# Attention plus gated expert on one Trainium2 core: expert matmuls in 128x32 column strips behind value passes, four products in one PSUM bank

## The chip, the cores and the metric

The kernel runs on one core of one Trainium2 chip, in one launch. The metric is the device time of one execution in microseconds (us); it is given as the median of several runs. The profile is that of one execution.

## The reference

Inputs are `q`, `k` and `v` of shape (8 batches, 12 heads, 448 tokens, 64) and two weights, `w_in` (768 x 2048) and `w_out` (2048 x 768), all in float32.

```
scores = q k^T / 8          per batch and head, 448 x 448
attn   = softmax(scores)
x      = attn v             heads side by side: 3584 tokens x 768
h      = x w_in             3584 x 2048
g      = h * sigmoid(h)
out    = g w_out            3584 x 768, float32
```

## The kernel before

All matmuls are in float16, with float32 sums in PSUM. The kernel is one long list of instructions whose order is made at build time: a planner (`Order`, with `Op`s that carry an estimated duration, dependences and a bias) plays the five engines forward and writes down what each does next. Rings (`Ring`) stand for buffers: an operation may start when a ring has a free entry. Each engine then works through its own list strictly in order, and waits on semaphores where data or a buffer is not ready. TensorE (PE) chooses between three kinds of work: score passes (`run_qk`), value passes (`run_av`) and a list `moe` of expert matmuls, of which any ready one among the first 24 may go.

Three shapes of matmul use the 128x128 array differently.

- **Scores** (`scores`, `scores_rest`, L336): contraction over 32 rows, so four heads run side by side in row tiles (32 x 128). A score pass has 8 matmuls of 448 columns (two rounds of four). ScalarE (ACT) takes the exponential of the scores (`expo`, L373).
- **Value passes** (`attend`, `attend_sums`, L399 and L415): output over 32 columns of the array, so four heads run side by side in column tiles (128 x 32). From the second batch on, units (a batch and a group of four heads) go in pairs. Part 0 sums the exponentials; parts 1 and 2 give the even and the odd half of the head dimension. A pair has three chunks of keys of its own for each unit, and one chunk in which the lower 64 rows belong to one unit and the upper 64 to the other ("the rest", 64 x 32 tiles). In each of parts 1 and 2 the own chunks come first and the shared chunk last: six rounds of four matmuls and one round of eight.
- **Expert matmuls** use the whole array: `ffn1` (L496, `h = x w_in`, six matmuls of 448 columns for each of 16 slices `f` of the 2048), `plain` (L718, the first four output tiles), `product` (L704) and `pair_product` (L632).

The second expert matmul is done for two tiles of 128 tokens at a time (a "quad", `queue_quad`) by Strassen's scheme: seven products of half size instead of eight. The inputs of the products are sums of quarters of `g` (`combine_g`, L694, on VectorE, DVE) and of `w_out` (`combine_w`, L533). Each product is eight matmuls of 384 columns. Products 3 and 5, 4 and 2, and 1 and 7 share a PSUM bank (the later one adds on top), product 6 has its own. `take_3`, `take_5` and `take_2` are copies on ACT (L770, L776, L780); `take_4`, `take_1`, `less_12`, `less_21`, `take_6` and `take_7` are additions on DVE (L766). Finished tiles lie in `ost` buffers (four) and are stored by SyncE's queue, in part by ACT's towards the end.

The first expert matmul of the last two batches is done by a seven-product scheme too (`queue_pair`, `pair_product`): for each of eight `f`, products 1, 6, 7, 5, 2, 3, 4 of three matmuls each. Its inputs are sums of `x` (`combine_x`, `sx`, L590) and of `w_in` (`combine_w_in`, `tw`, L608), its results are added on DVE (`pair_add`, L663), copied on ACT (`pair_copy`, L657) and gated on ACT (`silu`, L670). The buffer of `sx` 3 is the one that held `V` of the last batch. The normalised `x` of a value pass is written by DVE (`norm`, L482).

What a batch needs before its `ffn1` or its pair stage may run is the `norm` of its last value pass. Up to there the planner fills PE with products of older quads.

Of the kernel before, what the change touches and what calls it, by code (L numbers as in the profile page):

```python
# [165 lines left out]
def kernel(  # L166
# [36 lines left out]
    SHY = 0.5  # L203
    FAR = (NT * B // 4 - 3, NT * B // 4 - 1)
# [4 lines left out]
    NSG, NTMP, NOST = 3, 3, 4  # L209
# [213 lines left out]
    def attend(ns, part):  # L423
        made = []
        lone = len(ns) == 1
        if part == 0 and not lone:
            attend_sums(ns)
            return
        for n in ns:
            a = ps.tile([128, 512], FP32, name=f"a_{n}_{part}", tag="m", bufs=4)  # L430
            made.append(a)
            acc[(n, part)] = a
            for c in range(NCH if lone else NCH - 1):
                for h in range(HG):
                    attend_mm(
                        a, n, part, c, h, 0, rows_of(n, c), E[(n, c // per_burst(n))],
                        c == 0, lone and c == NCH - 1,
                    )
        if not lone:
            for h in range(HG):  # L440
                for i, n in enumerate(ns):
                    attend_mm(
                        made[i], n, part, 3, h, 64 * i, 64 * (i + 1), E[(ns[0], 3)],
                        False, True,
                    )

# [43 lines left out]

    h_t, th_t, o_t = {}, {}, {}

    def ffn1(b, f, t0, t1):
        h = ps.tile([128, 512], FP32, name=f"h_{b}_{f}_{t0}", tag="m", bufs=4)
        for cc in range(NDC):
            nc.tensor.matmul(  # L496
                out=h[:, 0 : t1 - t0],
                lhsT=w_in_t[:, cc, 128 * f : 128 * (f + 1)],
                rhs=x3(b, cc)[:, cc % 3, t0:t1],
                start=(cc == 0),  # L500
                stop=(cc == NDC - 1),
            )
        h_t[(b, f, t0)] = h
# [13 lines left out]
    W_ = {m: const.tile([128, HF, OH], FP16, name=f"D{m}") for m in (1, 4, 6)}  # L517
# [5 lines left out]
    W_[3], W_[7], W_[5], W_[2] = B_[0, 1], B_[1, 0], B_[1, 1], B_[0, 0]  # L523

    def combine_w(m, f0, f1):
        i0, i1, op = {
            1: ((0, 0), (1, 1), ALU.add),
            4: ((1, 0), (0, 0), ALU.subtract),
            6: ((0, 0), (0, 1), ALU.add),
            3: ((0, 1), (1, 1), ALU.subtract),  # L530
            7: ((1, 0), (1, 1), ALU.add),
        }[m]
        nc.vector.tensor_tensor(  # L533
            out=W_[m][:, f0:f1], in0=B_[i0][:, f0:f1], in1=B_[i1][:, f0:f1], op=op
# [76 lines left out]
    PBANK = {1: "A", 2: "A", 6: "B", 5: "C", 3: "C", 7: "D", 4: "D"}  # L611

    def pair_product(f, m):
        if m in (1, 5):
            pp_t[(f, PBANK[m])] = ps.tile(
                [128, 512], FP32, name=f"f_{f}_{m}", tag="m", bufs=4
            )[:, 0:S]
        elif m == 6:
            two = ps.tile([128, 2, 512], FP32, name=f"f_{f}_{m}", tag="s", bufs=2)
            pp_t[(f, "B")], pp_t[(f, "D")] = two[:, 0, 0:S], two[:, 1, 0:S]  # L620
# [10 lines left out]
        for c in range(3):  # L631
# [4 lines left out]
                start=(c == 0 and m in (1, 6, 5, 7)),  # L636
# [4 lines left out]
    def pair_tmp(f, name):  # L641
# [4 lines left out]
            "v": ("T", NT_, [128, HG, S], FP16),  # L646
# [4 lines left out]
        elif len(shape) == 3:  # L651
            t = t.rearrange("p h s -> p (h s)")
# [6 lines left out]
    def pair_add(f, to, x, y):  # L659
        x = pp_t[(f, x)] if x in "BCD" else pf_t[(f, x)]  # L660
        y = pf_t[(f, y)]
        out = pf_t[(f, to)] if (f, to) in pf_t else pair_tmp(f, to)
        nc.vector.tensor_tensor(out=out, in0=x, in1=y, op=ALU.add)  # L663
# [13 lines left out]
    S_t, tmp_t, ost_t, pr_t = {}, {}, {}, {}  # L677

    def combine_g(qd, m, f0, f1):
        a, b = 2 * qd, 2 * qd + 1  # L680
        x, y, op = {
            5: (rows(a, 0), rows(a, 1), ALU.add),
            2: (rows(b, 0), rows(b, 1), ALU.add),
            1: (rows(a, 0), rows(b, 1), ALU.add),
            6: (rows(b, 0), rows(a, 0), ALU.subtract),
            7: (rows(a, 1), rows(b, 1), ALU.subtract),
        }[m]
        if m > 5:
            dst = x
        else:  # L690
            if (qd, m) not in S_t:
                S_t[(qd, m)] = sb.tile([128, HF, 128], FP16, name=f"S_{qd}_{m}", tag="S", bufs=NSG)
            dst = S_t[(qd, m)]
        nc.vector.tensor_tensor(out=dst[:, f0:f1], in0=x[:, f0:f1], in1=y[:, f0:f1], op=op)  # L694

    BANK = {3: 3, 5: 3, 4: 4, 2: 4, 1: 1, 7: 1, 6: 6}

    def product(qd, m):
        w = {3: rows(2 * qd, 0), 4: rows(2 * qd + 1, 1), 6: rows(2 * qd + 1, 0), 7: rows(2 * qd, 1)}
# [3 lines left out]
        for f in range(HF):  # L703
            nc.tensor.matmul(  # L704
                out=pr_t[(qd, BANK[m])][:, 0:OH],
                lhsT=w[:, f, :],
                rhs=W_[m][:, f, :],
                start=(f == 0 and BANK[m] == m),
                stop=(f == HF - 1),
                skip_group_check=True,  # L710
            )


    def plain(t, j, f0, f1):
        if f0 == 0:
            pr_t[("o", t, j)] = ps.tile([128, 512], FP32, name=f"o_{t}_{j}", tag="m", bufs=4)
        for f in range(f0, f1):
            nc.tensor.matmul(  # L718
                out=pr_t[("o", t, j)][:, 0:OH],
                lhsT=rows(t, f // HF)[:, f % HF, :],  # L720
                rhs=B_[f // HF, j][:, f % HF, :],
                start=(f == 0),
                stop=(f == NFF - 1),
                skip_group_check=True,
# [8 lines left out]

    def tmp(qd, name):
        tmp_t[(qd, name)] = sb.tile([128, OH], FP32, name=f"{name}_{qd}", tag="tmp", bufs=NTMP)
        return tmp_t[(qd, name)]
# [28 lines left out]
    def add(out, a, b, op=ALU.add):  # L765
        nc.vector.tensor_tensor(out=out, in0=a, in1=b, op=op)  # L766


    def take_3(qd):
        nc.scalar.copy(out=tmp(qd, "s"), in_=bank(qd, 3))  # L770

    def take_4(qd):
        add(tmp_t[(qd, "s")], bank(qd, 4), tmp_t[(qd, "s")])

    def take_5(qd):
        nc.scalar.copy(out=ost(qd, 0, 1), in_=bank(qd, 3))  # L776
        store(qd, 0, 1)

    def take_2(qd):
        nc.scalar.copy(out=ost(qd, 1, 0), in_=bank(qd, 4))  # L780
        store(qd, 1, 0)

    def take_1(qd):
        add(tmp(qd, "m"), bank(qd, 1), tmp_t[(qd, "s")])

    def less_12(qd):
        add(tmp_t[(qd, "s")], tmp_t[(qd, "s")], ost_t[(qd, 0, 1)], ALU.subtract)

    def less_21(qd):
        add(tmp_t[(qd, "m")], tmp_t[(qd, "m")], ost_t[(qd, 1, 0)], ALU.subtract)  # L790

    def take_6(qd):
        add(ost(qd, 1, 1), bank(qd, 6), tmp_t[(qd, "m")])
        store(qd, 1, 1)

    def take_7(qd):
        add(ost(qd, 0, 0), bank(qd, 1), tmp_t[(qd, "s")])
        store(qd, 0, 0)
# [113 lines left out]
    sg_ring, tmp_ring, ost_ring = Ring(NSG), Ring(NTMP), Ring(NOST)  # L912
    far_ring = Ring(NX3)
    STORE = 3.0
    pr_op, sg_op, w_op, plain_op = {}, {}, {2: [], 5: []}, {}
    inv_op, norm_op = [], []
    quads = []

    def queue_ffn1(b, g0, g1):
        t0, t1 = 32 * g0, 32 * g1  # L920
        for f in range(NFF) if b == 0 else [x for f in range(HF) for x in (f, f + HF)]:

            def run(f=f):
                op = Op("PE", NDC * mm(t1 - t0), lambda: ffn1(b, f, t0, t1), tail=PE_OUT)
# [4 lines left out]
                od.on_pe(op, "full")  # L929
# [14 lines left out]
            def deps(f=f):  # L944
# [3 lines left out]
                for qd in range(NT * B // 4) if u else ():  # L948
                    if any(t // NT == u - 1 and (r or t % NT < 4) for t in (2 * qd, 2 * qd + 1)):
# [3 lines left out]
                            else [pr_op.get((qd, m)) for m in (3, 4, 6, 7)]  # L953
# [56 lines left out]
    def queue_pair_f(f, xs):  # L1010
        done, lo = {}, f // 4 * 4

        def free(r):
            made = []
            for qd in range(NT * B // 4):
                for t in (2 * qd, 2 * qd + 1):
                    if t // NT == PB // 2 - 1 and t % NT < (4, NT - 1)[r]:
                        made += [pr_op.get((qd, m)) for m in (3, 4, 6, 7)]
# [10 lines left out]
        def queue(m):  # L1029
            rings = {  # L1030
                1: ((rq_ring, 1),),
                6: ((s_ring, 1), (kt_ring, 1), (t_ring, 1)),
                5: ((rk_ring, 1),),
            }.get(m, ())
            ms = (6, 7) if m == 6 else (m,)

            def run():
                op = Op(
                    "PE",
                    3 * len(ms) * mm(S),  # L1040
                    lambda: [pair_product(f, x) for x in ms],
                    tail=PE_OUT,
                )
                if m in (1, 5):
# [7 lines left out]
                elif m == 6:  # L1052
                    read("u", "DVE", lambda: pair_add(f, "u", "B", "p"), [op, done["p"]])
                    read("v", "DVE", lambda: pair_add(f, "v", "D", "u"), [op, done["u"]])
                elif m == 5:
                    read("q", "ACT", lambda: pair_copy(f, "q", "C"), [op], None, -3)
                    read("22", "DVE", lambda: pair_add(f, "v", "q", "v"), [done["v"], done["q"]], rk_ring.give)
                    gate_of(1, 1, "v", [done["22"]], t_ring.give)
                elif m == 2:
                    gate_of(0, 0, "A", [op], m_ring.give)  # L1060
                elif m == 3:
                    read("12", "DVE", lambda: pair_add(f, "p", "C", "u"), [op, done["u"]], m_ring.give)
                    gate_of(1, 0, "p", [done["12"]], rq_ring.give)
                else:
                    read("21", "DVE", lambda: pair_add(f, "u", "D", "u"), [op, done["12"]], s_ring.give)
                    gate_of(0, 1, "u", [done["21"]], kt_ring.give)

            def deps():
                made = [xs[0, c] for c in (range(3, NDC) if m == 2 else range(3))]
                if m in (5, 6):  # L1070
                    made += [pair_x[i] for i in ((2, 3) if m == 6 else (1,))]
# [512 lines left out]
```

## Time and profile before

| | |
|---|---|
| time, median of 3 runs | 396.12 us (396.03 to 396.42) |
| span of the profiled execution, first to last instruction | 394.4 us |
| PE busy | 386.5 us (98%) |
| DVE busy | 311.3 us (79%) |
| ACT busy | 243.2 us (62%) |
| mean granted TensorE clock | 0.998 |
| bytes moved, mean | 87 GB/s |

The profiled execution is known by its span, 394.4 us; the median of the runs stands 1.7 us above it, for what lies before the first and behind the last instruction. In the timeline a row gives the start and the length of a run of equal instructions; the next row's start minus this row's start is what the run took of PE's time, since ends overlap the next start. Matmul names are output<-inputs, then the part of the array in use (128*128 whole, 32*128 row tile, 128*32 column tile), then the moving operand.

### The profile page before, as it was taken

How to read it: one execution, taken by the hardware profiler on the slowest of the kernel's cores; microseconds unless marked ns; L12 is line 12 of the kernel's file. 1: busy time of each engine (PE TensorE's matmuls, PEld its weight loads, DVE VectorE, ACT ScalarE, POOL GpSimd, SP SyncE). 2: the span in 40 equal slices, each digit the busy share in tenths (PEclk: the TensorE clock that was granted, in tenths of full speed). 3: DMA queues.
4: the chain of work that ended last, by engine and by line, in shares of the span. 5: the costliest groups of instructions: out<-in, count | busy, mean ns of one | idle time of the engine just before them, and what ended most of it. 6: DMA issues, size and time to landing. Idle time of an engine off the chain costs nothing.

```text
span 394.4 us, 9273 instructions
## 1 busy us (share of the span) xinstructions
PE 386.5 (98%) x3679; PEld 199.0 (50%) x3679; DVE 311.3 (79%) x653; ACT 243.2 (62%) x378; POOL 83.6 (21%) x153
## 2 busy tenths in 40 slices
PE   7999999999999999999999999999999999999995
PEld 6667764443444444554444444344444555556663
DVE  2466676999999697896888786988879898787863
ACT  4988885696863868626868429686593227872110
POOL 6632546315004242500051221120000000000000
PEclk9999999999999999999999999999999999999999
DMA  7999999919034863582145751531100131001334
GB/s 113 205 210 210 166 179 164 175 36 141 1 76 88 142 95 47 75 158 71 25 49 81 139 109 46 71 48 42 42 1 2 40 87 35 2 1 42 80 82 121
DMA packets 35356, 34.44 MB, mean 87 GB/s; under 512 B 11376, under 2 KB 33776, under 8 KB 35312
## 3 DMA queue, kind: packets, MB, share of 16 engines
q0 software_dynamic: 24784, 22.82, 39.2%
q1 hardware_dynamic: 9952, 10.33, 9.6%
q10 hardware_dynamic: 576, 0.69, 0.6%
q8 instruction: 29, 0.48, 0.5%
q14 instruction: 15, 0.12, 0.1%
HBM read 45.61 MB, written 11.01 MB: 144 GB/s over the span
## 4 chain that ended last, share of the span: by engine, by line
PE 94%; DMA 3%; DVE 1%; ACT 1%; POOL 0%; issue 0%; POOLq 0%
PE p L704 29%; PE h L496 29%; PE s L336 12%; PE a L399 10%; PE f L632 8%; PE o L718 3%; DMA rq<-in_q_dram 3%; PE a L415 2%; PE z L1491 1%; ACT E L373 0%; DVE S L694 0%; POOL rk L249 0%; DVE rq L323 0%; DVE rdn L466 0%; DVE ost L766 0%
## 5 line engine op out<-in xcount | busy, mean ns | idle before, releaser
L373 ACT ACTIVATE E<-s 128x896 f16<-128x896 f32 (+1 forms) x172 | 150.0, 915 | 48.6 <-PE s L336 47.5
L496 PE MATMUL h<-xT,w_in_t 128*128 128x448 f16 (+1 forms) x672 | 118.6, 327 | 0.0
L496 PEld LDWEIGHTS <-w_in_t 128*128 128x128 f16 x672 | 61.2, 98 | 54.0 <-issue 18.0
L507 ACT ACTIVATE th<-h 128x448 f16<-128x448 f32 (+1 forms) x112 | 54.3, 495 | 31.4 <-PE h L496 22.5
L543 DVE SCALAR_TENSOR_TENSOR G<-th,h 128x448 f16<-128x448 f16 (+2 forms) x112 | 55.1, 507 | 15.3 <-ACT th L507 13.3
L270 POOL DMA_DIRECT2D V<-in_v_dram x88 | 48.5, 568 | 56.5 <-PE a L399 42.7
L336 PE MATMUL s<-rq,KT 32*128 32x448 f16 (+4 forms) x768 | 50.9, 337 | 1.4 <-DVE rq L323 0.9
L704 PEld LDWEIGHTS <-G 128*128 128x128 f16 x384 | 36.5, 98 | 28.1 <-issue 4.4
L704 PEld LDWEIGHTS <-S 128*128 128x128 f16 x312 | 29.3, 98 | 23.9 <-issue 5.2
L399 PE MATMUL a<-E,V 128*32 128x448 f16 (+3 forms) x864 | 40.4, 335 | 0.0
L255 POOL DMA_DIRECT2D rq<-in_q_dram x27 | 15.1, 560 | 113.0 <-PE s L336 82.9
L704 PE MATMUL p<-D,G 128*128 128x384 f16 x208 | 37.6, 326 | 0.0
L704 PE MATMUL p<-w_out_t,S 128*128 128x384 f16 x208 | 37.2, 326 | 0.1
L482 DVE SCALAR_TENSOR_TENSOR xT<-a,rdn 128x448 f16<-128x448 f32 (+1 forms) x54 | 28.7, 565 | 7.4 <-PE a L399 6.5
L336 PEld LDWEIGHTS <-KT 32*128 32x128 f16 (+2 forms) x864 | 17.5, 98 | 29.6 <-issue 25.9
L704 PE MATMUL p<-w_out_t,G 128*128 128x384 f16 x176 | 31.9, 326 | 0.0
L399 PEld LDWEIGHTS <-V 128*32 128x32 f16 (+2 forms) x864 | 18.2, 95 | 22.4 <-issue 14.7
L384 DVE TENSOR_TENSOR T<-T,E 128x1792 f16<-128x1792 f16 x20 | 21.8, 1089 | 8.0 <-ACT E L373 7.9
L694 DVE TENSOR_TENSOR S<-G 128x512 f16<-128x512 f16 x70 | 25.3, 414 | 3.2 <-PE p L704 3.0
L384 DVE TENSOR_TENSOR T<-E,E 128x1792 f16<-128x1792 f16 x20 | 21.6, 1082 | 5.6 <-ACT E L373 5.6
L776 ACT COPY ost<-p 128x384 f32<-128x384 f32 x13 | 6.2, 480 | 27.4 <-PE p L704 22.6
L305 DVE STREAM_TRANSPOSE KT<-rk 128x256 f32<-128x256 f32 (+3 forms) x48 | 16.6, 384 | 7.0 <-DMA rk<-in_k_dram 6.2
(74 smaller groups left out, 370.2 us busy)
## 6 DMA issues: line engine op xcount, KB each, us to landing
out_dram<-ost SPq DMA_DIRECT2D x194, 48.0 KB, 1.7
rk<-in_k_dram POOLq DMA_DIRECT2D x24, 224.0 KB, 5.9
rq<-in_q_dram POOLq DMA_DIRECT2D x21, 224.0 KB, 5.2
w_in_t<-in_moe_w_in_dram POOLq DMA_DIRECT2D x6, 512.0 KB, 11.2
w_out_t<-in_moe_w_out_dram POOLq DMA_DIRECT2D x4, 768.0 KB, 13.5
V<-in_v_dram POOLq DMA_DIRECT2D x43, 64.0 KB, 3.9
V<-in_v_dram POOLq DMA_DIRECT2D x40, 48.0 KB, 4.0
out_dram<-ost SPq DMA_DIRECT2D x8, 96.0 KB, 2.2
```

What stands on the lines that cost most here:

```text
L270: nc.gpsimd.dma_start(out=VT[b][32 * x : 32 * (x + 1), hs, 0:count, :], in_=v[b, hs].rearrange("h (i g) d -> i h g d", g=TPP)[:, :, first ...
L336: nc.tensor.matmul(out=pS[p0 : p0 + 32 * (x1 - x0), h % 2, at : at + nq], lhsT=KT[(b, hg)][32 * h : 32 * (h + 1), c, x0:x1, :, e], rhs=QT[ ...
L373: nc.scalar.activation(out=E[(n, w)][0:kr, 2 * y : 2 * y + 2, 0:nk], in_=pS_t[(n, w, y)][0:kr, :, 0:nk], func=AF.Exp, scale=attn_scale,)
L384: nc.vector.tensor_tensor(out=T[n], in0=T[n] if step else E[(n, 0)], in1=E[(n, step + 1)], op=ALU.add,)
L399: nc.tensor.matmul(out=a[32 * h : 32 * (h + 1), 0:nq], lhsT=w, rhs=e[k0:k1, h, at : at + nq], start=start, stop=stop,)
L482: nc.vector.scalar_tensor_tensor(out=x3(b, cc)[:, cc % 3, 32 * g0 : 32 * g1], in0=acc[(n, part)][:, 0:nq], scalar=0.5, in1=rdn_t[n].rearra ...
L496: nc.tensor.matmul(out=h[:, 0 : t1 - t0], lhsT=w_in_t[:, cc, 128 * f : 128 * (f + 1)], rhs=x3(b, cc)[:, cc % 3, t0:t1], start=(cc == 0), s ...
L507: nc.scalar.activation(out=th, in_=h_t[(b, f, t0)][:, 0 : t1 - t0], func=AF.Tanh)
L543: nc.vector.scalar_tensor_tensor(out=dst[:, f, at + lo : at + hi], in0=th_t[(b, f, t0)][:, lo - t0 : hi - t0], scalar=1.0, in1=h_t[(b, f, ...
L632: nc.tensor.matmul(out=pp_t[(f, PBANK[m])], lhsT=w[:, c, :], rhs=a[:, c, :], start=(c == 0 and m in (1, 6, 5, 7)), stop=(c == 2), skip_gro ...
L694: nc.vector.tensor_tensor(out=dst[:, f0:f1], in0=x[:, f0:f1], in1=y[:, f0:f1], op=op)
L704: nc.tensor.matmul(out=pr_t[(qd, BANK[m])][:, 0:OH], lhsT=w[:, f, :], rhs=W_[m][:, f, :], start=(f == 0 and BANK[m] == m), stop=(f == HF - 1),
```

## The change

1. **Strips.** A new helper `times` issues an expert matmul either whole or as four matmuls of 128 x 32, one for each strip of 32 output rows. `ffn1`, `plain` and `product` are issued in strips if the last thing on PE was in column tiles (`od.mode == "cols"`) and attention work is still left.
2. **Shared keys first in part 2.** The second value pass of a pair (part 2) begins with the shared chunk; part 1 still ends with it. A value pass thus ends in 128 x 32 tiles after part 2.
3. **Another scheme for the seven products** (Winograd's form). Products 1, 6, 7 and 4 of a quad add up in one PSUM bank and are read between; 5 and 3 share a second, 2 has a third. Sums of inputs build on each other (5, then 6, then 3 and, in place, 7). Out of PSUM go four copies on ACT (`take_copy`) and three additions on DVE (`take_sum`). Three `tmp` buffers go; `ost` has seven buffers instead of four. The pair stage does the same with half of an `s` tile for products 1, 6, 7, 4: order 1, 5, 6, 2, 7, 3, 4, three copies on ACT and three additions on DVE for each `f`.
4. **A value pass gives way** to an expert matmul if a score pass is due within 0.8 us (`AWAIT`).

```diff
+    AWAIT = 0.8
-    NSG, NTMP, NOST = 3, 3, 4
+    NSG, NOST = 3, 7
...
+        if not lone and part == 2:
+            rest()
+        for i, n in enumerate(ns):
+            for c in range(NCH if lone else NCH - 1):
...
+        if not lone and part == 1:
+            rest()
...
+    def times(out, w, x, start, stop, strips):
+        cut = 32 if strips else 128
+        for i in range(0, 128, cut):
+            nc.tensor.matmul(
+                out=out[i : i + cut],
+                lhsT=w[:, i : i + cut],
+                rhs=x,
+                start=start,
+                stop=stop,
+                skip_group_check=True,
+            )
...
-            5: (rows(a, 0), rows(a, 1), ALU.add),
-            2: (rows(b, 0), rows(b, 1), ALU.add),
-            1: (rows(a, 0), rows(b, 1), ALU.add),
-            6: (rows(b, 0), rows(a, 0), ALU.subtract),
-            7: (rows(a, 1), rows(b, 1), ALU.subtract),
+            5: (rows(b, 0), rows(b, 1), ALU.add),
+            6: (S_t.get((qd, 5)), rows(a, 0), ALU.subtract),
+            7: (rows(a, 0), rows(b, 0), ALU.subtract),
+            3: (rows(a, 1), S_t.get((qd, 6)), ALU.subtract),
...
-    BANK = {3: 3, 5: 3, 4: 4, 2: 4, 1: 1, 7: 1, 6: 6}
+    BANK = {1: 1, 6: 1, 7: 1, 4: 1, 2: 2, 5: 5, 3: 5}
...
+    OUT = {1: (0, 0), 5: (1, 1), 6: (0, 1), 4: (1, 0)}
+    SUM = {2: (0, 0), 7: (1, 1), 3: (0, 1)}
+    def take_copy(qd, m):
+        nc.scalar.copy(out=ost(qd, *OUT[m]), in_=bank(qd, BANK[m]))
+        if m == 4:
+            store(qd, *OUT[m])
+    def take_sum(qd, m):
+        t = ost_t[(qd, *SUM[m])]
+        nc.vector.tensor_tensor(out=t, in0=bank(qd, BANK[m]), in1=t, op=ALU.add)
+        store(qd, *SUM[m])
...
-    PBANK = {1: "A", 2: "A", 6: "B", 5: "C", 3: "C", 7: "D", 4: "D"}
+    PBANK = {1: "A", 6: "A", 7: "A", 4: "A", 2: "B", 5: "C", 3: "C"}
...
-        for m in (1, 6, 5, 2, 3, 4):
+        for m in (1, 5, 6, 2, 7, 3, 4):
             queue(m)
...
+                strips = od.mode == "cols" and bool(qk_seq or av_seq)
-                od.on_pe(op, "full")
+                od.on_pe(op, "cols" if strips else "full")
...
-        od.on_pe(op, "cols")
+        od.on_pe(op, "rest cols" if two and part == 2 else "cols")
         if two and part:
-            od.mode = "rest cols"
+            od.mode = ("rest cols", "cols")[part - 1]
...
-                if av is not None and av <= od.now - 0:
+                soon_qk = qk is not None and units[qk_seq[0][0][0]][0] > 0
+                soon_qk = soon_qk and max(qk, pace["next"]) < od.now + AWAIT
+                if av is not None and av <= od.now and not soon_qk:
                     run_av()
```

## Prediction

> **What bounds the kernel now.** I read the page first, its busy table and the chain that ended last.
>
> ```profile
> PE 386.5 (98%) x3679; PEld 199.0 (50%) x3679; DVE 311.3 (79%) x653; ACT 243.2 (62%) x378; POOL 83.6 (21%) x153
> PE 94%; DMA 3%; DVE 1%; ACT 1%; POOL 0%; issue 0%; POOLq 0%
> ```
>
> PE sets the end: only what shortens PE's list, or makes PE wait, moves the time. Next, the timeline of PE where the three kinds of matmul alternate, and in the pair stage, where only one kind runs.
>
> ```profile
> 131.28 0.57 PE L336 MATMUL s<-rq,KT 32*128 32x448 f16 x8
> 131.79 2.44 PE L496 MATMUL h<-xT,w_in_t 128*128 128x448 f16 x12
> 134.17 0.57 PE L336 MATMUL s<-rq,KT 32*128 32x448 f16 x8
> ...
> 144.03 3.20 PE L399 MATMUL a<-E,V 128*32 128x448 f16 x64
> 147.16 1.31 PE L496 MATMUL h<-xT,w_in_t 128*128 128x448 f16 x6
> ...
> 330.04 1.86 PE L632 MATMUL f<-sx,tw 128*128 128x448 f16 x9
> 331.74 1.30 PE L632 MATMUL f<-xT,w_in_t 128*128 128x448 f16 x6
> ```
>
> With no change of tile shape, nine whole matmuls take 331.74 - 330.04 = 1.70 us, 0.189 each. The twelve at 131.79 should take 2.27 but take 2.38: a change of shape costs 0.11. The score pass is two rounds of four, 0.38, and takes 0.51: 0.13. The 64 matmuls at 144.03 are two value passes of seven rounds, 14 x 0.189 = 2.65, and take 3.13: 0.48 for four changes (into the rest, out, into it again, out to whole): 0.12 each. So a change costs 0.10 to 0.12 us, wherever it stands, on PE.
>
> Last, the place where value passes end and the pair stage begins, on PE and on DVE.
>
> ```profile
> 306.20 1.63 PE L399 MATMUL a<-E,V 128*32 128x448 f16 x32
> 307.77 1.47 PE L704 MATMUL p<-w_out_t,S 128*128 128x384 f16 x8
> 309.81 1.46 PE L704 MATMUL p<-D,S 128*128 128x384 f16 x8 [0.57 <-ACT ost L780]
> 311.12 2.77 PE L704 MATMUL p<-D,G 128*128 128x384 f16 x16
> ```
>
> ```profile
> 307.93 0.86 DVE L590 TENSOR_TENSOR sx<-xT,xT 128x1344 f16<-128x1344 f16 x1 [1.00 <-PE a L399]
> 308.71 1.82 DVE L608 TENSOR_TENSOR tw<-w_in_t 128x1536 f16<-128x1536 f16 x2
> 310.45 1.15 DVE L482 SCALAR_TENSOR_TENSOR xT<-a,rdn 128x448 f16<-128x448 f32 x2
> 311.51 0.94 DVE L608 TENSOR_TENSOR tw<-w_in_t,tw 128x1536 f16<-128x1536 f16 x1
> ...
> 318.53 0.85 DVE L590 TENSOR_TENSOR sx<-xT,xT 128x1344 f16<-128x1344 f16 x1
> ```
>
> The last value pass ends at 307.83. DVE starts `sx` 3 only then (its buffer is the `V` that the pass reads), and the last two `norm`s stand behind it and two `tw`: 2.6 us late. PE does not feel that, since it has ten products (307.77 to 322.66) in front of most pair work; it stands 0.73 (eight products take 8 x 0.163 = 1.30 from 307.77, the next starts at 309.81).
>
> **Changes of shape.** The order of instructions on PE has 258 changes of tile shape before and 233 after: column to whole 25 to 6, whole to row 71 to 52, column to row 16 to 35, between column tiles and the rest 26 to 20, whole to column tiles (rest included) 13 to 13; the others stay. 25 x 0.105 = -2.6 us (bounds -2.5 and -3.0). All of it is on PE, which never waits long, so it counts in full unless PE then waits.
>
> **Strips.** 1,000 strip matmuls, 250 rounds, take the place of 250 whole matmuls. No row has an expert matmul in strips; the nearest are value passes: 0.189 a round at 448 columns like a whole one, and at 224 columns
>
> ```profile
> 31.61 0.95 PE L399 MATMUL a<-E,V 128*32 128x224 f16 x32
> 32.49 1.32 PE L496 MATMUL h<-xT,w_in_t 128*128 128x224 f16 x12
> ```
>
> eight rounds in 0.88 with one change, 0.096 a round; twelve whole ones take 1.26 with one change, also 0.096. So I take 0; the bounds are 0 and, at 0.003 a round from reading error, +0.7. The Trainium skill (TensorEngine Tiling (Array Packing), Restrictions) says that column tiling turns the fast weight load off, and TensorE: Matmul & The Clock Gate, LDWEIGHTS, gives 1/1.2 ns a column: 107 ns for four strips, which by estimate would slow only the 60 rounds of 224 columns, by 11 ns, +0.7 us in all. The trace speaks against it: 96 ns with four loads a round.
>
> **Fewer sums.** On DVE: quad additions 78 to 39 (L766, 548 ns), sums of `g` 130 to 104 (L694, 415), pair additions 40 to 24 (L663, 623), sums of `w_out` 10 to 8 (943): -44 us. On ACT: quad copies 39 to 52 (480 ns) and pair copies 16 to 24 (530): +10.5 us. Neither is on the path; 0. In the pair stage ACT gets three copies (starts 0.43 apart) and four silus (0.47 apart) per `f`, 3.2 us, while PE needs 21 x 0.189 = 3.97: it stays under. The order leaves two products (1.13 us) between two writers of the shared bank there; copy and lag need 0.7. Without that cover it would be 0.2 x 24 reads = 5 us. Stores and loads keep number and queue. At the end, a copy of 0.48 takes the place of the last addition of 0.56: -0.1, which I leave out.
>
> **Where the pair stage begins.** This is what speaks against a gain. The order after has no product left between the last value pass and the pair stage: PE goes on with pair products 1, 1, 2, 2 (of two `f`), then 5, which needs `sx` 1. On DVE the list is `sx` 3 (still waiting for the value pass), `tw`, `tw`, `norm`, `norm`, two pair additions, `sx` 1. Counted from the end of the pass (307.83 above): `sx` 3 at 0.10, the `norm`s at 2.62, the next operation at 3.68, two pair additions at 0.53 each to 4.75, `sx` 1 takes 0.85 to 5.60, and product 5 starts at 5.65. PE starts 0.06 before the pass's end and has four products of 0.567: ready at 2.2. Idle 3.45. Then 5 three times, 6, 6, 7: 7 stands one product (0.57) behind 6, whose copy on ACT needs 0.16 lag + 0.53 + hops = 0.75: 0.2 more. +3.65, and the old 0.73 goes: +2.9. Behind that wait stand the whole pair stage and the last quads: nothing gives it back. Bounds: +0.3 if DVE gets through two steps sooner than its list says, +4.5 if `norm`s and copies are late too.
>
> **Other waits.** Of the stalls elsewhere before, 0.27 hangs on DVE's sums (222.21, sixteen products in 3.04 where 2.77 is the rule); with 11 us less sums I take -0.2. A new order has new ones: 0, bounds -0.5 and +1.5.
>
> **Sum.** -2.6 + 0 + 2.9 - 0.2 = +0.1 us on a span of 394.4. The median stands 1.7 above the span, and what lies outside is not touched: 396.2 us. A measurement of this kernel tells about 0.2%, 0.8 us, from no change.
>
> **Rivals.**
> 1. *The start of the pair stage is covered* (faster). If PE waits about as long there as before, -2.6 - 0.2 stays: 393.3; with 1.2 us of the hole left, 394.5. For: the planner expected the `norm`s in time, and all rows in my walk are short. Against: DVE's list is fixed, and the trace shows `sx` 3 waiting for just this value pass. Chance 0.25.
> 2. *Waits of the bank that four products share* (slower). A quad's copy must be over before the next product adds to the bank. ACT works in order: a copy (0.48) that becomes ready behind two exponentials (0.92 each) ends 0.35 + 1.83 + 0.48 = 2.66 after its product, and where one product and a score pass lie between, 1.87, PE waits 0.8. In the order after, 13 of 52 such places have 1.9 or less (10 of 39 before, without a stall like that). It decides from the second hit on: two to four hits give 397.8 to 399.4. Chance 0.2.
> 3. *The clock drops in the 3.45 us hole* (slower). In the kernel's first microseconds the zero matmuls run at half rate, 29 in 3.0 us (0.103 each) where later ones take 0.055. Half rate for 3 us again would cost 1.5: 397.7. No row before has a hole over 0.9 us, so the trace shows neither. Chance 0.1. The Trainium skill (TensorE: Matmul & The Clock Gate, What's actually happening) has the clock halved after an idle window of 3.4 us that runs freely: a hole of 3.45 would just miss it nearly always.
> 4. That strips run one after another is excluded by the value passes' rows.
>
> **How the numbers follow.** Forecast 0.45, spread 395.3 to 397.1 (walk +0.5, other waits -0.5 to +0.7). The range reaches over rival 1 and most of 2 and 3: 393.3 to 398.4. Faster by over 0.2%, below 395.3: rival 1 and a little of the forecast, 0.27. Within: 0.41. Slower, above 396.9: rivals 2 and 3 and the forecast's edge, 0.32.
>
> **What would show it.** Right: a score pass after strips starts with no more than one change behind the value pass; rows of `h` and `p` on 128*32 at 0.189 and 0.163 a round; a hole of some 3.4 us on PE in front of the first `f<-sx,tw`, released by DVE `sx`; DVE near 267 us busy, ACT near 254. Wrong: no such hole (rival 1), many gaps of PE in front of L503 products released by ACT (rival 2), a granted clock below 1 behind the hole (rival 3), or rounds of strips above 0.2.

## The result, and the profile after

The changed kernel takes 398.57 us (median of 4 runs, 398.49 to 399.08) where the kernel before takes 396.07 (4 runs, 395.67 to 396.42): a ratio of 1.0069, 95% interval 1.0056 to 1.0082. It is slower by 2.5 us. The forecast was 396.2, and the range's upper end was 398.4. The profiled executions have spans of 396.7 and 394.4 us. Two executions on record, one of the kernel before (413.32 us) and one of experiment 3 (411.19 us), ran at a mean granted clock near 0.95 and are left out everywhere.

The busy table and the summary of the chain that ended last, of the kernel after:

```profile
PE 385.3 (97%) x4429; PEld 202.3 (51%) x4429; DVE 275.1 (69%) x570; ACT 252.7 (64%) x399; POOL 83.7 (21%) x153
PE 96%; DVE 1%; DMA 1%; issue 1%; ACT 0%; DVEq 0%; POOLq 0%
```

PE still sets the end. It has 750 more matmuls (250 matmuls became four strips each) and yet less busy time, while the span is longer: the loss is in gaps, and busy time also hides matmuls that run too slowly. DVE lost 36 us and ACT gained 9.5, and neither moved the end.

The place where the value passes end and the pair stage begins, first on PE, then on DVE (start, length, engine, line, operation, count, idle time before and its releaser):

```profile
312.97 1.47 PE L503 MATMUL p<-w_out_t,S 128*32 128x384 f16 x32
314.27 1.62 PE L400 MATMUL a<-E,V 128*32 128x448 f16 x32
...
317.23 1.63 PE L400 MATMUL a<-E,V 64*32 64x448 f16 x32
318.79 2.44 PE L652 MATMUL f<-xT,w_in_t 128*128 128x448 f16 x12
324.46 5.48 PE L652 MATMUL f<-sx,tw 128*128 128x448 f16 x18 [3.22 <-DVE sx L611]
329.77 0.73 PE L652 MATMUL f<-sx,w_in_t 128*128 128x448 f16 x3
```

```profile
318.92 0.86 DVE L611 TENSOR_TENSOR sx<-xT,xT 128x1344 f16<-128x1344 f16 x1 [1.80 <-PE a L400]
319.69 1.82 DVE L629 TENSOR_TENSOR tw<-w_in_t 128x1536 f16<-128x1536 f16 x2
321.43 1.15 DVE L491 SCALAR_TENSOR_TENSOR xT<-a,rdn 128x448 f16<-128x448 f32 x2
322.50 1.14 DVE L678 TENSOR_TENSOR p<-f,p 128x448 f32<-128x448 f32 x2
323.56 0.84 DVE L611 TENSOR_TENSOR sx<-xT,xT 128x1344 f16<-128x1344 f16 x1
```

The hole is there, in front of the first `f<-sx,tw`, released by DVE's `sx`. The twelve matmuls at 318.79 take 12 x 0.19 = 2.28, so PE is ready at 321.07 and stands 3.39 until 324.46. DVE's list is the one that the prediction walked through: `sx` 3, two `tw`, two `norm`s, two pair additions, `sx` 1. What the walk did not have is in the next row: eighteen matmuls from 324.46 take 329.77 - 324.46 = 5.31 us, where 18 x 0.189 = 3.40 is the rule and 0.22 of a wait belongs to it. The two stretches, in the hole and behind it (stretch, length; then busy time and count of PE, PEld, DVE, ACT, POOL; then the granted clock of PE, the DMA share and GB/s):

```profile
320.00:324.40 4.40, 1.24 (x7) 0.43 (x5) 4.40 (x8) 1.74 (x4) 0.00 (x0) 1.00 0.26 68
324.40:328.50 4.10, 4.04 (x13) 1.75 (x14) 3.28 (x5) 1.60 (x3) 0.00 (x0) 0.58 0.00 0
```

The granted clock is 0.58 behind the hole, as a mean over 4.10 us: the clock's record has 0.50 for 3.41 us, from 325.00 to 328.41, and 1.00 on both sides. In these 3.41 us matmuls start 0.374 apart instead of 0.189. That costs half of 3.41, 1.7 us, and the row says the same: 5.31 - 3.40 - 0.22 = 1.69.

And one place that the prediction had not looked at, in the timeline of PE at the first strips:

```profile
31.84 0.27 PE L503 MATMUL h<-xT,w_in_t 128*32 128x224 f16 x4
33.85 1.24 PE L503 MATMUL h<-xT,w_in_t 128*32 128x224 f16 x44 [1.74 <-issue]
35.02 0.57 PE L337 MATMUL s<-rq,KT 32*128 32x448 f16 x8
```

The first round of strips runs, then nothing for 1.9 us (33.85 - 31.84 is 2.01, a round is 0.10). The releaser is "issue": no semaphore explains it. The other 44 strips need 35.02 - 33.85 = 1.17 with the change of shape, as whole matmuls would.

The account of the two profiled executions, in us:

| | |
|---|---|
| 25 fewer changes of shape at 0.109 | -2.7 |
| the hole in front of the pair products | +3.4 |
| the wait of product 7 behind product 6 | +0.2 |
| half clock behind the hole | +1.7 |
| stall at the first strips | +1.9 |
| stalls of before that are gone: 0.73 at 309.81, 0.27 at 222.21, 0.42 at 53.19 | -1.4 |
| the first 10 us, which differ from one execution to the next | -0.4 |
| the end behind the last matmul, 4.51 before and 4.28 after | -0.2 |
| sum | +2.5 |

The spans differ by 2.3 and the medians by 2.5, so some 0.2 us of small differences between the two executions are not placed. Two entries were not in the forecast: the half clock, which was a rival with a chance of 0.1, and the stall at the first strips, which was nowhere.

### The profile page after: what moved, and what is told of

It is laid out like the page before. It is cut to its first block, busy times and chain, and to the rows that moved or that the text cites. A ratio compares the mean times of both kernels' runs of the same rounds, so it can differ in the third digit from the quotient of the medians.

```text
span 396.7 us, 10765 instructions
## 1 busy us (share of the span) xinstructions
PE 385.3 (97%) x4429; PEld 202.3 (51%) x4429; DVE 275.1 (69%) x570; ACT 252.7 (64%) x399; POOL 83.7 (21%) x153
## 4 chain that ended last, share of the span: by engine, by line
PE 96%; DVE 1%; DMA 1%; issue 1%; ACT 0%; DVEq 0%; POOLq 0%
PE p L503 30%; PE h L503 29%; PE s L337 13%; PE a L400 11%; PE f L652 8%; PE o L503 3%; PE a L416 2%; DMA rk<-in_k_dram 1%; PE z L1474 1%; DVE xT L491 0%; DVE p L678 0%; ACT E L374 0%; DVE sx L611 0%; DVE KT L306 0%; ACT u L674 0%
## 5 line engine op out<-in xcount | busy, mean ns | idle before, releaser
L503 PE MATMUL h<-xT,w_in_t 128*128 128x448 f16 (+3 forms) x1122 | 119.0, 322 | 1.7 <-issue 1.7
L503 PEld LDWEIGHTS <-w_in_t 128*32 128x32 f16 (+1 forms) x1122 | 63.3, 97 | 53.7 <-issue 15.9
L776 ACT COPY ost<-p 128x384 f32<-128x384 f32 x52 | 25.0, 481 | 65.5 <-PE p L503 62.0
L503 PEld LDWEIGHTS <-G 128*128 128x128 f16 (+1 forms) x580 | 42.9, 98 | 32.5 <-issue 5.6
L503 PE MATMUL p<-w_out_t,G 128*128 128x384 f16 (+1 forms) x328 | 49.2, 326 | 0.0
L503 PEld LDWEIGHTS <-S 128*128 128x128 f16 (+1 forms) x456 | 30.1, 97 | 22.3 <-issue 3.1
L503 PE MATMUL p<-D,S 128*128 128x384 f16 (+1 forms) x232 | 37.0, 326 | 0.0
L782 DVE TENSOR_TENSOR ost<-p,ost 128x384 f32<-128x384 f32 x39 | 21.5, 553 | 20.4 <-PE p L503 15.1
L652 PE MATMUL f<-sx,tw 128*128 128x448 f16 x72 | 18.3, 381 | 3.3 <-DVE sx L611 3.2
```

What stands on the lines that cost most here:

```text
L503: nc.tensor.matmul(out=out[i : i + cut], lhsT=w[:, i : i + cut], rhs=x, start=start, stop=stop, skip_group_check=True,)
L652: nc.tensor.matmul(out=pp_t[(f, PBANK[m])], lhsT=w[:, c, :], rhs=a[:, c, :], start=(c == 0 and m in (1, 2, 5)), stop=(c == 2), skip_group_ ...
L776: nc.scalar.copy(out=ost(qd, *OUT[m]), in_=bank(qd, BANK[m]))
L782: nc.vector.tensor_tensor(out=t, in0=bank(qd, BANK[m]), in1=t, op=ALU.add)
```

## The experiments

The questions were: what is the stall at the first strips (column tiles themselves, or the number of instructions), does the clock drop hang on the hole and how much is it worth, is the hole made by DVE's fixed list, and is what is left of the change the price of the shape changes? The kernel before gave medians of 396.08 and 396.09 beside the two groups of runs (first four, then four more experiments).

**1. The first batch's `ffn1` whole again**

```diff
-lambda: ffn1(b, f, t0, t1, strips)
+lambda: ffn1(b, f, t0, t1, strips and b > 0)
```

> The changed kernel, its order of instructions kept, but the first batch's first expert matmuls (ffn1, 60 rounds of four strips of 224 columns) are issued whole. Theory A (PE ran out of instructions at 33.85 us: strips make 8 instructions per 0.096 us, and while the loads saturate the DMA engines a new block of 256 instructions comes every 5.9 us at best): the stall of 1.9 us at 33.85 goes, 5 more changes of shape cost 0.5, so 398.6 - 1.9 + 0.5 = 397.2 us. Rival (PE waited there for the x of the first batch or for its weights): the stall stays with whole matmuls, 398.6 + 0.5 = 399.1 us.

Measured: median 397.23 (395.45 to 397.74, 12 runs), ratio 1.0015 (1.0000 to 1.0030). In PE's timeline of this kernel the stall is gone:

```profile
32.41 1.32 PE L503 MATMUL h<-xT,w_in_t 128*128 128x224 f16 x12
33.67 0.57 PE L337 MATMUL s<-rq,KT 32*128 32x448 f16 x8
```

Twelve matmuls take 33.67 - 32.41 = 1.26. The hole is kept, 3.39. The median hides two groups: seven executions at 397.1 to 397.7 with a mean granted clock of 0.995 to 0.996, and five at 395.5 to 395.9 with 0.999 (means 397.5 and 395.6). So behind the same hole the clock drops in some executions and not in others, and the groups lie 1.9 us apart (the trace of the changed kernel shows 1.7). That the median meets the expected 397.2 is luck: the expectation had the drop in it, and the executions with the drop stand at 397.5. In the changed kernel all four runs show 0.995 or 0.996. Stall and drop together bring the changed kernel from 398.6 to 395.6, and that with five shape changes more.

**2. `norm`s first at the start of the pair stage**

```diff
+            if f0 == 4 and 1 not in pair_x:
+                return
...
-                    [pair_w[(k, f0)] for k in {2: (1,), 4: (2,)}.get(m, ())],
+                    [pair_w[(k, f0)] for k in {2: (1,), 4: (2,)}.get(m, ())]
+                    + ([pair_x[1]] if f0 == 4 else []),
...
-            made = made + [pair_x[k] for k in {2: (1,), 4: (2,)}.get(m, ())]
+            made = made + [pair_x[k] for k in {2: (1,), 3: (1,), 4: (2,)}.get(m, ())]
```

`sx` 3, which waits for the value pass, and the `tw` of the second half now come behind `sx` 1 in DVE's list.

> The changed kernel, but sx 3 and the late tw of the pair stage may only start after sx 1, so that the last two norms stand first on DVE behind the last value pass. Theory B (the hole of 3.4 us in front of pair product 5 comes from DVE's list, where the norms stand behind sx 3, which waits for V, and the half clock behind it comes from the hole): product 5 can start some 1.6 us after the pass, before PE is through with the four products in front of it; the hole (3.4), the clock's drop (ten matmuls at 0.374 in place of 0.189, 1.85) and the 0.2 behind it go: 398.6 - 5.4 = 393.2 us. If the hole only moves to product 6 or 7: 395 to 397. Rival (the slow matmuls have another cause, such as DVE's reading beside them): 398.6 - 3.6 = 395.0, with granted clock still near 0.6 for 4 us.

Measured: 393.30 (393.23 to 394.81, 6 runs), ratio 0.9937 (0.9922 to 0.9951). PE, then DVE, at the start of the pair stage:

```profile
320.39 2.44 PE L652 MATMUL f<-xT,w_in_t 128*128 128x448 f16 x12
322.67 3.57 PE L652 MATMUL f<-sx,tw 128*128 128x448 f16 x18
```

```profile
319.94 1.19 DVE L491 SCALAR_TENSOR_TENSOR xT<-a,rdn 128x448 f16<-128x448 f32 x2 [1.24 <-PE a L400]
321.17 0.86 DVE L611 TENSOR_TENSOR sx<-xT,xT 128x1344 f16<-128x1344 f16 x1
```

The twelve matmuls go over into the eighteen without a gap (322.67 - 320.39 = 2.28), since the `norm`s now start while the last value pass still ends and `sx` 1 is over at 322.03. That gives back 5.3 us: hole 3.4, clock 1.7, and the 0.2 of product 7. The profiled execution is the slowest of the six, 394.81: it stands 2.19 us at 33.9, at the first strips, and the clock from 35.0 to 38.3 is 0.50. The other five, at 393.2 to 393.5, show mean clocks of 0.998 to 1.0. So a hole of 2.2 us dropped the clock too, in one execution of six; this execution is 1.5 above the median.

**3. Zero matmuls in the hole**

```diff
+        if m == 5 and f == 0:
+            for _ in range(56):
+                nc.tensor.matmul(
+                    out=spare[0], lhsT=zeros, rhs=zeros, start=True, stop=True
+                )
```

PE works through the hole instead of standing; the zeros go to an unused half of an `s` tile. Nothing becomes ready sooner.

> The changed kernel with 56 matmuls of zeros (128 columns, 0.055 us each, 3.1 us in all) on PE in front of the first pair product 5, that is, in the hole; nothing else is changed. Theory B1 (the clock drops because PE idles for 3.4 us): the hole is filled, product 5 starts when it did, and the ten slow matmuls run at 0.189: 398.6 - 1.85 = 396.7 us. Rival (the matmuls there are slow because DVE or ACT works beside them, or because the operands were just written): no change, 398.6 us.

Measured: 397.18 (396.82 to 397.76, 7 runs), ratio 1.0029 (1.0019 to 1.0040).

```profile
319.59 2.44 PE L660 MATMUL f<-xT,w_in_t 128*128 128x448 f16 x12
321.87 3.29 PE L656 MATMUL f<-zeros 128*128 128x128 f16 x56
325.26 3.79 PE L660 MATMUL f<-sx,tw 128*128 128x448 f16 x18
```

The eighteen matmuls take 3.63 (to 328.89) instead of 5.31, 1.7 less, and the granted clock in the 4 us from 325.0 is 1.00. Product 5 starts as late as in the changed kernel, 5.67 behind the first pair product (325.26 - 319.59 here, 324.46 - 318.79 there), so at this place nothing differs but the clock. The median falls by 1.4 and not by 1.7; the 0.3 are not placed, but this profiled execution is 0.67 behind the changed kernel's already at 9.7 us, long before the zeros. The clock drop thus hangs on PE being idle, not on what follows.

**4. The kernel before, with its first `ffn1` cut in two**

```diff
+            cut = (t1 - t0) // 2 if b == 0 else t1 - t0
+            for i in range(0, t1 - t0, cut):
...
-                rhs=x3(b, cc)[:, cc % 3, t0:t1],
+                    rhs=x3(b, cc)[:, cc % 3, t0 + i : t0 + i + cut],
```

Matmuls of 224 columns become two of 112, of the whole array: twice the instructions and no column tile. The first batch's sums are not the reference's here.

> The kernel before, with each of the first batch's ffn1 matmuls of 224 columns cut into two of 112: no strips, same tile shape, same columns, twice the instructions. Theory A (instruction supply): a block of 254 weight loads and matmuls, begun at 28.4 us, would be used up by 32.9 instead of 34.3, so PE stalls 1.4 us there for nothing that the profile shows: 396.1 + 1.4 = 397.5 us. Rival (the stall belongs to column strips): within 0.3 us of before, 396.1 to 396.4, by the small cost of more matmuls.

Measured: 397.43 (397.13 to 397.86, 5 runs), ratio 1.0037 (1.0025 to 1.0049), 1.35 more than the kernel before.

```profile
32.13 0.96 PE L498 MATMUL h<-xT,w_in_t 128*128 128x112 f16 x16
33.92 0.55 PE L498 MATMUL h<-xT,w_in_t 128*128 128x112 f16 x8 [0.82 <-issue]
```

The same kind of stall, at the same time, in a kernel without a single expert strip. It is the number of instructions, not the tiles. The stall is 1.0 us, where 1.4 was expected; the other part of the 1.35 is about what 192 more matmuls take (60 halves take 3.05 where 30 whole ones take 2.97). So the time came out as expected from two costs, and not from the stall alone. Where the instructions come from is seen in the DMA records: instructions are loaded in packets of 16 KB on a queue of their own (35 packets after, 29 before), which from 20 to 40 us start 5.9 us apart in both kernels, at 20.14, 26.09, 31.98 and 37.92 before and at 19.69, 25.66, 31.54 and 37.46 after. In these stretches the other loads keep the DMA engines full (the DMA share is 0.8 or more in every slice from 31 to 36). PE stops after the 952nd and the 1,207th of its weight loads and matmuls, 255 apart, and goes on 2.2 to 2.5 us after such a packet starts. Before, it stands 0.39 at the first of these places, at 28.41, too; it comes to the second only at 34.3, when the block is just there (31.98 + 2.3). After, the strips bring it there at 31.94. The packets follow what PE uses up: later in the kernel before they start 12 to 14 us apart (45.28, 57.74, 71.73). In all ten traces the next packet starts 3.4 to 3.8 us after PE has passed one of the two places, so 5.9 us reads as the time from the call for a block until PE can use it; this is inferred and was not tried.

**5. `norm`s first, and strips only from 38 us of the planner's time on**

```diff
-                strips = od.mode == "cols" and bool(qk_seq or av_seq)
+                strips = od.mode == "cols" and od.now > 38 and bool(qk_seq or av_seq)
```

(in all three places, beside the edit of experiment 2; 235 changes of shape).

> The kernel with the norms first (as in the run of that name), and strips only from 38 us of the planner's time on, when the heavy loads are over. 235 changes of shape instead of 233. Theory A and B together: neither the hole nor the stall for instructions is left; 393.3 - 1.9 (up to 2.3 where the clock drops behind that stall) + 0.2 = 391.2 to 391.6 us. Rival: the stall for instructions moves to the first strips after 38 us: 392.5 to 393.3.

Measured: 392.39 (392.15 to 392.77, 4 runs), ratio 0.9907 (0.9893 to 0.9920). The stall for instructions does not come: the 72 strips at 44.51, when loads have become lighter, take 1.83, 0.102 a round with the change of shape behind them. The time misses the expectation by 0.8. The planner's order changed with the edit, and PE has a new wait of 0.84 for a `norm` at 97.14.

```profile
44.51 1.90 PE L503 MATMUL h<-xT,w_in_t 128*32 128x224 f16 x72
46.34 0.57 PE L337 MATMUL s<-rq,KT 32*128 32x448 f16 x8
...
97.14 1.29 PE L503 MATMUL h<-xT,w_in_t 128*128 128x448 f16 x6 [0.74 <-DVE xT L491]
```

**6. `norm`s first, the first batch whole, order kept** (experiments 1 and 2 together, 238 changes of shape)

> The kernel with the norms first and the first batch's ffn1 whole, order kept: 238 changes of shape. Theory A and B: 393.3 - 1.9 + 0.5 = 391.9 us; 0.3 above the kernel with strips from 38 us on, for three more changes of shape.

Measured: 391.95 (391.56 to 392.62, 4 runs), ratio 0.9896 (0.9883 to 0.9910). It has the lowest median of all, and beats both kernels: 6.6 us under the changed kernel, 4.1 under the one before. It stands 0.4 below experiment 5, where 0.3 above was expected: the wait of 0.84 does not occur in its order.

**7. `norm`s first, no strips at all** (`cut = 128` in `times`, same order as experiment 6; 258 changes of shape, as many as before)

> The kernel with the norms first, its order kept, all expert matmuls whole: 258 changes of shape, as many as in the kernel before, while shared keys first and the other scheme of products stay. Theory C (each change of shape costs 0.10 us of PE and strips cost nothing by themselves): 23 changes more than the kernel with strips from 38 us on, so 391.4 + 2.4 = 393.8 us. Rival (a part of the gain is lost in the strips' own weight loads): less than 2 us above it.

Measured: 394.12 (5 runs), ratio 0.9950 (0.9938 to 0.9963). Against experiment 6 that is 2.17 us for 20 changes of shape, 0.109 each. Against experiment 5, which the expectation named, it is only 1.73, and under 2 was the rival's sign; but experiment 5 has another order and its wait of 0.84, and only experiment 6 has the order of this kernel. One such place, in the timeline of PE, first without strips, then in experiment 6:

```profile
91.41 0.36 PE L416 MATMUL a<-E,both 128*32 128x448 f16 x4
91.70 2.44 PE L503 MATMUL h<-xT,w_in_t 128*128 128x448 f16 x12
94.08 0.57 PE L337 MATMUL s<-rq,KT 32*128 32x448 f16 x8
```

```profile
90.74 0.36 PE L416 MATMUL a<-E,both 128*32 128x448 f16 x4
90.93 2.44 PE L503 MATMUL h<-xT,w_in_t 128*32 128x448 f16 x48
93.30 0.58 PE L337 MATMUL s<-rq,KT 32*128 32x448 f16 x8
```

The round ahead takes 0.29 in front of whole matmuls and 0.19 in front of strips; twelve whole matmuls and twelve rounds of strips then take the same, 2.38 and 2.37. Strips save the change and cost nothing else here.

**8. The kernel before, with `norm`s first**

The edit is that of experiment 2, in the kernel before.

> The kernel before with the norms first in the pair stage. If the 0.73 us that PE stands at 309.81 hangs on the late norms and what stands behind them on DVE, 396.1 - 0.7 = 395.4 us. If the ten products cover it and the stand has another cause (the bank that a copy frees), 396.1 us, no change.

Measured: 395.50 (11 runs), ratio 0.9985 (0.9976 to 0.9994), 0.6 less. The stand of 0.73 at 309.81 is gone: the next eight matmuls follow the first eight after 1.31.

```profile
307.24 1.48 PE L704 MATMUL p<-w_out_t,S 128*128 128x384 f16 x8
308.55 1.46 PE L704 MATMUL p<-D,G 128*128 128x384 f16 x8
```

So the old order hid nearly all of the late `norm`s behind its ten products, and the changed one had nothing to hide them.

From before to experiment 6 the steps are -0.6 (`norm`s first, 396.09 to 395.50), -1.4 (the rest of the changed kernel, without strips, to 394.12) and -2.2 (20 shape changes less, to 391.95). The step of 1.4 is between two kernels with 258 changes and `norm`s first each. Which part of it belongs to the other product scheme, to the shared keys and to the small stalls of another order was not tried; their profiled spans differ by only 0.6, and 0.4 of that is the end behind the last matmul (4.63 and 4.26).

## Why the prediction was wrong

**Changes of shape: right.** 25 x 0.105 was forecast; a change is 0.109 by experiments 6 and 7.

**The walk through DVE's list: right.** It had `sx` 1 ready 5.60 after the pass and product 5 at 5.65; in the trace the pass ends at 318.86 and product 5 starts at 324.46, 5.60 after. The hole was 3.39 for 3.45, product 7's wait 0.22 for 0.2, and the old stall of 0.73 went. Rival 1, a covered start, did not occur; experiment 2 shows what it would have been worth.

**Fewer sums and the shared bank: right in what matters.** No wait of PE for the bank that a quad's four products share stands in the trace (rival 2), and neither DVE nor ACT decides. ACT's 252.7 is near the 254 forecast; DVE's 275 is 8 above the 267. The counts came out as forecast (39 quad additions, 104 sums of `g`, 24 pair additions), but I took off the full lengths of rows, and back to back they overlap: two pair additions at 322.50 have 1.14 and take 1.06, so 83 instructions less save some 0.05 to 0.1 each less than their lengths.

**Strips: wrong.** The term was 0, with bounds 0 and +0.7, and this is the first step that failed. The rate of a round was right: 0.189, 0.163 and 0.096 us at 448, 384 and 224 columns. But I costed a strip as time in the array alone, and took four instructions for one as free. At the first batch, rounds of 224 columns need eight instructions in 0.1 us while the loads keep the DMA engines full, and PE ran out of instructions: +1.9 us. The row was there before the change: the wait for "issue" that the kernel before has at 28.41, in PE's timeline.

```profile
28.41 0.28 PE L399 MATMUL a<-E,ones 96*32 96x224 f16 x3 [0.23 <-issue]
```

It stands among value passes of 224 columns, which use up instructions as fast as the strips do, and I passed over it as too short.

**The clock behind the hole: wrong in its chance, near in its price.** This is the second step that failed. Rival 3 had 1.5 us and a chance of 0.1. It measured 1.7 and came in all four runs of the changed kernel, and in 7 of 12 of experiment 1 behind the same hole. I set the chance by a rule rather than by a row, since no row before has such a hole: the Trainium skill (TensorE: Matmul & The Clock Gate, What's actually happening) has an idle window of 3.4 us that runs freely. The traces agree with the window: in all ten, the clock changes only at whole steps of 3.41 us from its first rise, which comes 4.0 to 7.0 us into the execution. What failed is the reading that the hole must fill such a step: steps in which PE idled for 59% or more were followed by half clock, and steps with 54% or less were not, as the table at the end shows. So a hole of 2 to 3.4 us can be enough, depending on where it falls. By the mean clocks, the drop came in 11 of the 16 executions with this hole.

**The sum.** Taken away from 398.6, the two missed entries of 1.9 and 1.7 leave 395.0, 1.2 under the forecast; experiment 1's faster group, 395.6 with five changes more, says the same. Of that, 1.0 lies in the account's rows that I had not counted: the stall at 53.19, the first 10 us, and the end behind the last matmul, of which I had left out 0.1. So the forecast of "no change" would have been too high by itself, and the two missed costs both came on top of the hole.

## What to carry to other kernels

A change of tile shape on TensorE costs 0.11 us here, and column strips avoid it at no cost in array time; but they quadruple the instructions, so count instructions per microsecond where loads fill the DMA engines, and look for short "issue" waits before you add more. Walk an engine's fixed list at each change of stage: one operation that waits for a buffer, put ahead of the urgent ones, cost 3.4 us here, and setting it back was worth 5.3. A hole on TensorE of some 2 us or more should be given the price of a clock drop behind it, 1.7 us here, with a chance, and not only its own length.

## What the runs showed of the hardware

- While the loads filled the DMA engines, 16 KB packets of instructions came 5.9 us apart, each good for 255 weight loads and matmuls: some 43 a microsecond. Faster use ended in stalls of 0.39, 1.9, 2.19 and 1.0 us (before and after, after, experiment 2, experiment 4). That the loads are what slows the packets is inferred from the place of the stalls and from their absence at the 72 strips later on; it was not tried by moving loads.
- The clock is halved behind a hole of 3.39 us in most executions and behind one of 2.19 us in one of six; a matmul of 448 columns then takes 0.374 instead of 0.189, and it lasts one step of 3.41 us.
- The share of a step in which PE idles separates the two cases in all ten traces. Steps are 3.41 us long and counted from the first rise of the clock. The table has the steps nearest to the border; every step with more idle time, at the end of an execution, was followed by half clock, and every one with less by full clock. What share would be needed between 54% and 59% no trace shows.

| run | step, us | PE busy in it, us | PE idle | clock in the next step |
|---|---|---|---|---|
| experiment 1 | 319.76 to 323.17 | 0.42 | 88% | 0.50 |
| changed kernel | 321.58 to 325.00 | 0.54 | 84% | 0.50 |
| experiment 8 | 387.79 to 391.20 | 0.81 | 76% | 0.50 |
| experiment 4 | 389.74 to 393.15 | 1.36 | 60% | 0.50 |
| experiment 2 | 31.47 to 34.88 | 1.40 | 59% | 0.50 |
| experiment 7 | 386.79 to 390.20 | 1.56 | 54% | 1.00 |
| changed kernel | 31.45 to 34.86 | 1.67 | 51% | 1.00 |
| experiment 6 | 383.91 to 387.32 | 1.85 | 46% | 1.00 |

A hole of 3.39 us that is split evenly between two steps leaves each at some 50%. That would explain why the same hole drops the clock in some executions only; no execution without the drop was profiled behind that hole.
